# P times v of a pooled attention in eighths of the TensorE array, in float32

## The chip, the cores and the metric

The kernel runs on one core of a Trainium2 chip. The metric is the device time of one execution in microseconds (us); the comparison takes the median of several runs. A core has TensorE (PE; its weight loads are PEld), VectorE (DVE), ScalarE (ACT), GpSimd (POOL) and SyncE (SP), which here issues nearly all transfers. Each engine has its own instruction stream and waits for others by semaphores.

## The reference

Eight batches of attention with eight heads, 576 queries and head dimension 64; keys and values are first averaged over groups of eight positions, so a head has 72 keys. Behind the attention stands a chain of products with weights on all 4608 tokens.

```python
k_p = k.reshape(B, H, 72, 8, 64).mean(axis=3)
v_p = v.reshape(B, H, 72, 8, 64).mean(axis=3)
scores = scale * np.matmul(q, k_p.transpose(0, 1, 3, 2))
attn = softmax(scores)                     # float32
x = np.matmul(attn, v_p)                   # to (4608, 512): heads side by side
out = ((x @ w1) * (x @ w2)) @ w3 @ w_out   # w*: float64
```

## The kernel before

**The weights.** `w3 @ w_out` is formed once (`w_mm`, in 16 steps), which takes the first 85 us of the profiled execution. Every product with weights is done in float32r with a high and a low part of each operand: three passes (high x high, high x low, low x high), `PASSES`. `split` makes the parts: ScalarE casts the high part, VectorE (or GpSimd) subtracts.

**The chunks.** The 4608 tokens are done in 12 chunks of 384 (three tiles of 128). A batch has 576 tokens, so of three chunks one lies over two batches (`pieces` gives the parts: one of 384 columns, or two of 192). For chunk `m` the loop over `j` (8 column blocks) runs `a_mm` and `b_mm` (12 matmuls of 384 columns each, into the PSUM banks `a` and `b`), multiplies them (`b_post`), and `out_mm` adds their product with the folded weights into three banks `o0` to `o2` (9 matmuls of 512 columns). These five banks are the pool `pacc`; the other three are the pool `patt`, tag `att`, used by the whole attention.

**The attention of the next chunk** is threaded through the current one. `s_mm`: scores of a token tile, 16 float32 matmuls with 64 rows and 64 columns of weights, 72 columns streamed, into two `att` banks. `soft1`, `soft2`: row minimum, difference, exp, sum, normalise; for the tiles in `SOFT_ACT` ScalarE does exp with the minimum as bias and the sum as accumulator, otherwise VectorE subtracts first. The result `E` has, for a token, 8 heads x 72 keys. A pair of heads has 144 keys, which is over the 128 rows of the array: 128 of them are handled as a block per pair of heads, and the 2 x 8 that remain go into a small tile `R` (`soft3`), which holds their high and low parts twice each. For P transposed, chunks 0 and 1 use TensorE (`pt_mm`, `ptr_mm`, then `pt_post`, `ptr_post`), later ones VectorE transposes of 32 x 32 (`pt_turn`), a transfer that puts the blocks in place (`pt_move`) and a split into high and low (`pt_split`): `PTh` (high) and `PTx` (low parts, and the transposed `R`).

**The values.** `load_v` and `load_vr` load the pooled rows of v, `prep_v` and `prep_vr` add eight rows on GpSimd (`pool_tree`), and `prep_v2`, `prep_vr1`, `prep_vr2` make high and low parts in block-diagonal tiles `vbd` (two heads, 128 x 128) and `VR`.

**The product `av_mm(n, pr)`** takes one `att` bank for a pair of heads and runs four float32r matmuls with 128 rows into it for each piece:

```python
vh, vl = (vbd[b % 2][s][:, pr] for s in range(2))
nc.tensor.matmul(out=o, lhsT=vh, rhs=PTh[n][:, pr, c], start=True, stop=False)
nc.tensor.matmul(out=o, lhsT=vh, rhs=PTx[n][:, cc, pr], start=False, stop=False)
nc.tensor.matmul(out=o, lhsT=vl, rhs=PTh[n][:, pr, c], start=False, stop=False)
nc.tensor.matmul(out=o, lhsT=VR[b % 2][:, pr], rhs=PTx[n][:, cc, NPR + pr // 2], start=False, stop=True)
```

`av_post(n, pr)` splits the bank into the high and low parts of `xT`, the operand of `a_mm` and `b_mm` of the next chunk.

**The order** is written out by hand: `at(kind, k, fn, ...)` puts a call into slot `k`; a slot holds first loads (`L`), then elementwise work (`P`), weight products (`M`) and attention matmuls (`A`). A `j` step takes three slots, a chunk 24, beginning at `M0 + 24 * m`. Each engine runs its part in that order.

Of the kernel before, what the change touches and what calls it, by code (L numbers as in the profile page):

```python
# [19 lines left out]
def kernel(  # L20
# [55 lines left out]
    nc.vector.tensor_reduce(  # L76
        out=msk,
        in_=ident.rearrange("p (a two e) -> p two a e", two=2, e=2),
        axis=AX.XY,
        op=ALU.add,  # L80
    )
    nc.vector.tensor_tensor(out=msk[:, 0:1], in0=msk[:, 0:1], in1=msk[:, 1:2], op=ALU.subtract)
# [321 lines left out]
    def prep_v(b, hf):  # L404
        if hf == 0:
            vm[b] = p1.tile([P, NPR, D], F32, tag="vm", name="vm")
        pool_tree(stage.pop(("v", b, hf)), vm[b][:, 2 * hf:2 * hf + 2])
# [7 lines left out]
    def prep_vr(b):  # L415
        t = stage.pop(("vr", b))
        m = t[:, :, 0]
        pool_tree(t, m)
        stage["vrp", b] = m

    def prep_vr1(b):
        m = stage["vrp", b]
        hi = p1.tile([P, 2, D], F32R, tag="vrh", name="vrh")
# [4 lines left out]
        stage["vrp", b] = f(hi), m  # L428

    def prep_vr2(b):  # L430
        hi, m = stage.pop(("vrp", b))
        for r in range(4):
            rows = slice(32 * r, 32 * r + 32)
            par = r % 2
# [424 lines left out]
```

## Time and profile before

| | |
|---|---|
| median of 3 runs | 766.41 us (765.66 to 767.91) |
| the profiled execution | 766.73 us, its span 764.9 us |
| mean granted TensorE clock | 0.996 of full speed |
| TensorE busy | 745.8 us (98%) |
| VectorE, ScalarE, GpSimd busy | 443.0, 277.7, 193.2 us |

The span is what the profile shows of the execution. Matmuls are pipelined, so they overlap in the records: the time that one takes in a row of them is the distance of their starts, not their duration.

### The profile page before, as it was taken

Reading aid. Unit: us, or ns where it says so; the run is one execution under the profiler, and the core shown is the slowest. Engines: PE = TensorE matmul, PEld = TensorE weight load, DVE = VectorE, ACT = ScalarE, POOL = GpSimd, SP = SyncE. Lnnn points to the kernel's source line nnn. Section 1 sums busy time; section 2 is a strip of 40 time slices with the busy share of each in tenths; the row PEclk is TensorE's granted clock in tenths of the full one; section 3 lists DMA queues with packets and bytes.
Section 4 is the critical chain, followed back from the end, with each engine's and each line's share of the span. In section 5 each row is a group of like instructions: output and inputs, shape, how many; then the busy total and the mean of one; then the engine's idle time right before and its main releaser. Section 6 shows DMA issues by size and latency. Waiting matters only on the chain.

```text
span 764.9 us, 13065 instructions
## 1 busy us (share of the span) xinstructions
PE 745.8 (98%) x4998; PEld 681.5 (89%) x4998; DVE 443.0 (58%) x874; ACT 277.7 (36%) x670; POOL 193.2 (25%) x229
## 2 busy tenths in 40 slices
PE   8898989999999999999999999999999999999998
PEld 7676878999999999999899999999999899899997
DVE  6976877475485483475574573574574663662211
ACT  5567976232233332222233322232332332322211
POOL 1342666005208500006118500016038300000000
PEclk9999999999999999999999999999999999999999
DMA  9999920027144323037046223145154231210101
GB/s 316 334 286 226 316 37 1 1 79 140 45 122 103 93 84 63 7 109 149 27 116 144 66 59 55 42 95 127 44 136 117 74 67 28 63 42 1 42 1 41
DMA packets 123726, 74.52 MB, mean 97 GB/s; under 512 B 75408, under 2 KB 107408, under 8 KB 123664
## 3 DMA queue, kind: packets, MB, share of 16 engines
q1 hardware_dynamic: 123520, 73.56, 37.4%
q8 instruction: 39, 0.64, 0.4%
q14 instruction: 23, 0.19, 0.1%
q10 hardware_dynamic: 144, 0.13, 0.0%
HBM read 52.43 MB, written 9.44 MB: 81 GB/s over the span
## 4 chain that ended last, share of the span: by engine, by line
PE 84%; DVE 6%; DMA 4%; ACT 4%; issue 1%; SPq 1%; POOL 0%; ACTq 0%
PE a L611 25%; PE b L611 25%; PE o L651 25%; PE att L452 3%; DMA raw<-in_moe_w_out_dram 3%; DMA raw<-in_moe_w_dram 2%; PE att L586 1%; PE att L588 1%; ACT E L478 1%; PE att L587 1%; PE att L585 1%; PE o L681 1%; DVE wb L153 1%; ACT hl L157 1%; DVE hl L158 1%
## 5 line engine op out<-in xcount | busy, mean ns | idle before, releaser
L611 PE MATMUL a<-xT,hl 128*128 128x384 f32 x1152 | 220.4, 339 | 0.4 <-POOL hl L158 0.4
L611 PE MATMUL b<-xT,hl 128*128 128x384 f32 x1152 | 217.9, 337 | 1.9 <-DVE a L631 1.9
L611 PEld LDWEIGHTS a<-xT,hl 128*128 128x128 f32 x1152 | 200.2, 188 | 7.4 <-POOL hl L158 0.7
L611 PEld LDWEIGHTS b<-xT,hl 128*128 128x128 f32 x1152 | 202.0, 189 | 2.2 <-DVE a L631 2.2
L651 PE MATMUL o<-Wc,gh 128*128 128x512 f32 (+1 forms) x576 | 178.8, 391 | 0.0
L397 POOL TENSOR_TENSOR st<-st 128x512 f32<-128x512 f32 (+1 forms) x52 | 71.3, 1371 | 267.3 <-DMA st<-in_k_dram 227.6
L631 DVE TENSOR_TENSOR a<-b,a 128x384 f32<-128x384 f32 x96 | 52.8, 550 | 123.8 <-PE b L611 123.7
L651 PEld LDWEIGHTS o<-Wc,gh 128*128 128x128 f32 x576 | 106.5, 189 | 17.2
L651 PE MATMUL o<-Wc,gl 128*128 128x512 f32 (+1 forms) x288 | 113.2, 393 | 0.0
L632 ACT CAST gh<-a 128x384 fp32r<-128x384 f32 x96 | 49.3, 513 | 166.5 <-DVE a L631 166.5
L621 ACT COPY a<-a 128x384 f32<-128x384 f32 x96 | 45.8, 477 | 111.0 <-PE a L611 100.6
L637 DVE TENSOR_TENSOR gl<-a,gh 128x384 fp32r<-128x384 f32 x96 | 60.2, 627 | 12.8 <-ACT gh L632 12.8
L651 PEld LDWEIGHTS o<-Wc,gl 128*128 128x128 f32 x288 | 54.1, 188 | 12.3
L473 ACT ACTIVATE E<-E 128x288 f32<-128x288 f32 x64 | 28.4, 444 | 96.2 <-DVE E L470 96.1
L597 DVE TENSOR_TENSOR xT<-att,xT 128x384 fp32r<-128x384 f32 x48 | 26.6, 557 | 59.6 <-ACT xT L596 59.6
L474 DVE TENSOR_REDUCE sm<-E 128x4 f32<-128x288 f32 x64 | 29.0, 453 | 36.2 <-ACT E L473 36.2
L681 PE MATMUL o<-hl 128*128 128x512 f32 x144 | 40.6, 415 | 3.2 <-DVE hl L187 3.1
L158 DVE TENSOR_TENSOR PTx<-PTx,PTh 128x512 fp32r<-128x512 f32 x30 | 23.5, 783 | 33.1 <-ACT PTh L157 29.7
L398 POOL TENSOR_TENSOR st<-st 128x256 f32<-128x256 f32 (+1 forms) x52 | 41.3, 794 | 4.1
L413 POOL TENSOR_TENSOR vbd<-vm,vbd 64x256 fp32r<-64x256 f32 x16 | 12.4, 773 | 97.9 <-ACT vbd L412 97.4
L468 DVE TENSOR_REDUCE mx<-att 128x4 f32<-128x288 f32 x72 | 31.8, 442 | 8.8 <-PE att L452 8.8
L681 PEld LDWEIGHTS o<-hl 128*128 128x128 f32 x144 | 26.7, 194 | 9.4 <-DVE hl L187 4.1
(99 smaller groups left out, 774.9 us busy)
## 6 DMA issues: line engine op xcount, KB each, us to landing
raw<-in_moe_w_dram SPq DMA_DIRECT2D x32, 512.0 KB
PTx<-T SPq DMA_DIRECT2D x120, 96.0 KB
out_dram<-ob SPq DMA_DIRECT2D x35, 256.0 KB
st<-in_v_dram SPq DMA_DIRECT2D x16, 512.0 KB
st<-in_k_dram SPq DMA_DIRECT2D x28, 288.0 KB
qs<-in_q_dram SPq DMA_DIRECT2D x112, 48.0 KB
raw<-in_moe_w_out_dram SPq DMA_DIRECT2D x8, 512.0 KB
qs<-in_q_dram SPq DMA_DIRECT2D x96, 24.0 KB
```

The costliest lines, as they stand in the source:

```text
L158: eng.tensor_tensor(out=lo, in0=src, in1=f(hi), op=ALU.subtract)
L397: nc.gpsimd.tensor_tensor(out=t[:, :, 0:4], in0=t[:, :, 0:4], in1=t[:, :, 4:8], op=ALU.add)
L398: nc.gpsimd.tensor_tensor(out=t[:, :, 0:2], in0=t[:, :, 0:2], in1=t[:, :, 2:4], op=ALU.add)
L468: nc.vector.tensor_reduce(out=mx[:nt, hs], in_=sv, axis=AX.X, op=ALU.min)
L474: nc.vector.reduce_sum(out=sm[:nt, hs], in_=E[:nt, hs], axis=AX.X)
L611: nc.tensor.matmul(out=o, lhsT=w12[j, w][sw][:, kt * P:(kt + 1) * P], rhs=x[sx][:, kt], start=(i == 0), stop=(i == 3 * NK - 1))
L621: nc.scalar.copy(out=a, in_=gt[m, j][:, :CH])
L631: nc.vector.tensor_tensor(out=g, in0=ps[:, :CH], in1=g, op=ALU.mult)
L632: nc.scalar.copy(out=gh, in_=g)
L637: nc.vector.tensor_tensor(out=gl, in0=g, in1=f(gh), op=ALU.subtract)
L651: nc.tensor.matmul(out=oacc[m][t][x][:, cols], lhsT=(gh, gl)[sg][:, c], rhs=W[j][sw][:, cols], start=(j == 0 and i == 0), stop=(j == NJ - ...
L681: nc.tensor.matmul(out=wacc[h][it], lhsT=w3t[s][sa][:, it * P:(it + 1) * P], rhs=wo[j][sb], start=(j == 0 and i == 0), stop=(j == NJ - 1 a ...
```

## The change

The product runs in float32 on tiles of 32 rows and 64 columns of the array, eight of them. A head's 72 keys are three parts of 24, each in a row group of 32 (the rest of P is zero there, and v's rows beside it are whatever keys lie there). Four heads stand in the four row groups, and the heads 0 to 3 and 4 to 7 in the two column halves; so a chunk's product is 3 parts x 2 halves x 4 row groups = 24 matmuls for each piece. The four row groups go to four PSUM banks: bank `a` of `pacc` and all three of `att`. `av_mm(n)` is one call in one slot, and four `av_post` follow in the next.

P (the padded tile `EB`, two of them, zeroed once) and v (`vm`) stay in float32: `soft3`, `ptr_mm`, `ptr_post`, `pt_split`, `prep_v2`, `prep_vr`, `prep_vr1`, `prep_vr2` and the mask are gone. In chunks 0 and 1 the six transposes of a tile go in one slot, into two `att` banks (four and two), and are copied by ScalarE and VectorE. v is loaded as three parts of a batch, each by four transfers. The order of rows in `xT` is another (heads `4c + g` in column `g`), so w1 and w2 are loaded with rows permuted, each array by two transfers. Tile (0,1) leaves `SOFT_ACT`. `pt_turn` and `pt_move` come one slot earlier.

```diff
+    KS = 3
+    KW = KP // KS
+    KG = KW - 4
+    EW = 2 * P + 4
...
-    SOFT_ACT = [(0, 0), (0, 1), (0, 2), (1, 1)]
+    SOFT_ACT = [(0, 0), (0, 2), (1, 1)]
...
-    vbd = [[cp.tile([P, NPR, P], F32R, name=f"vbd{i}_{s}") for s in range(2)] for i in range(2)]
-    VR = [cp.tile([P, NPR, P], F32R, name=f"VR{i}") for i in range(2)]
-    msk = cp.tile([P, 2], F32, name="msk")
+    vm = [cp.tile([P, KS, 2, D], F32, name=f"vm{i}") for i in range(2)]
+    EB = [cp.tile([P, KS * EW], F32, name=f"EB{i}") for i in range(2)]
...
-        nc.sync.dma_start(
-            out=raw["w12", j, w].rearrange("p (k c) -> p k c", k=NK),
-            in_=(w1r, w2r)[w][:, 2 * j * P:2 * (j + 1) * P].rearrange("(k p) c -> p k c", p=P))
+        cols = (w1r, w2r)[w][:, 2 * j * P:2 * (j + 1) * P].rearrange("(c g d) x -> c d g x", c=2, g=NK)
+        for c in range(2):
+            nc.sync.dma_start(
+                out=raw["w12", j, w][D * c:D * c + D].rearrange("p (g x) -> p g x", g=NK), in_=cols[c])
...
+    def load_v(b, r):
+        t = stage["v", b, r] = st_tile([P, 2, POOL, D])
+        keys = v[b, :, KG * r * POOL:(KG * r + 32) * POOL].rearrange("(c g) (k e) d -> g k c (e d)", g=4, e=POOL)
+        for g in range(4):
+            nc.sync.dma_start(out=t[32 * g:32 * g + 32].rearrange("p c e d -> p c (e d)"), in_=keys[g])
...
-    def prep_v2(b, par):
-        r = slice(64 * par, 64 * par + 64)
-        hi, lo = (vbd[b % 2][s][r, :, D * par:D * par + D] for s in range(2))
-        nc.scalar.copy(out=hi, in_=vm[b][r])
-        nc.gpsimd.tensor_tensor(out=lo, in0=vm[b][r], in1=f(hi), op=ALU.subtract)
...
+    def prep_v(b, r):
+        pool_tree(stage.pop(("v", b, r)), vm[b % 2][:, r])
+    Et, Mt, PT, xT = {}, {}, {}, {}
+    def parts(E):
+        return E.rearrange("p (r x) -> p r x", x=EW)[:, :, :2 * P].rearrange("p r (h k) -> p h r k", k=32)[:, :, :, :KW]
...
+            Et[n, t] = EB[stage.setdefault("tiles", 0) % 2]
...
+                out=E, in0=sv,
+                in1=mx[:, hs].unsqueeze(2).unsqueeze(3).broadcast_to([P, 4, KS, KW]), op=ALU.subtract)
+            nc.scalar.activation(out=E, in_=E, func=AF.Exp, scale=-1.0)
+            nc.vector.tensor_reduce(out=sm[:, hs], in_=E, axis=AX.XY, op=ALU.add)
...
-        for dup in range(2):
-            nc.scalar.copy(out=R[:nt, :, :, :, dup, 0], in_=er)
-        for dup in range(2):
-            nc.vector.tensor_tensor(
-                out=R[:nt, :, :, :, dup, 1], in0=er, in1=f(R[:nt, :, :, :, dup, 0]), op=ALU.subtract)
...
+    def pt_mm(n, t, lo, hi):
         E = Et[n, t]
-        R = Rt[n, t] = p1.tile([P, NPR, 2, KR, 2, 2], F32R, tag="T" if (n, t) == (0, 1) else "R", name="R")
-        er = E[:nt].rearrange("p (a h) (x e) -> p a (h x) e", h=2, e=KR)[:, :, 0:18:17, :]
-        for dup in range(2):
-            nc.scalar.copy(out=R[:nt, :, :, :, dup, 0], in_=er)
-        for dup in range(2):
-            nc.vector.tensor_tensor(
-                out=R[:nt, :, :, :, dup, 1], in0=er, in1=f(R[:nt, :, :, :, dup, 0]), op=ALU.subtract)
-    Tp = {}
-    def pt_mm(n, t):
-        off, nt = t * P, P
-        E = Et[n, t].rearrange("p (a h) k -> p a (h k)", h=2)
         ps = patt.tile([P, 512], F32, tag="att", name="att")
-        pv = ps.rearrange("p (a c) -> p a c", c=P)
-        for pr in range(NPR):
-            nc.tensor.transpose(
-                out=pv[:, pr, :nt], in_=E[:nt, pr, KR:KR + P], identity=ident[:nt, :nt])
-        Tp[n, t] = pv
-    def ptr_mm(n, t):
-        off, nt = t * P, P
-        R = f(Rt[n, t].rearrange("p a h e u s -> p (a h e u s)"))
-        ps = patt.tile([P, 512], F32, tag="att", name="att")
-        rv = ps[:, :2 * P].rearrange("p (a c) -> p a c", c=P)
-        for g in range(2):
-            nc.tensor.transpose(
-                out=rv[:, g, :nt], in_=R[:nt, g * P:(g + 1) * P], identity=ident[:nt, :nt])
-        Tp[n, t, "r"] = rv
-    def pt_tiles(n):
-        PTh[n] = p1.tile([P, NPR, CH], F32R, tag="PTh", name="PTh")
-        PTx[n] = p1.tile([P, CH // 32, NPR + 2, 32], F32R, tag="PTx", name="PTx")
-    def pt_lo(n, c, w):
-        return PTx[n][:, c.start // 32:c.stop // 32, w].rearrange("p c a i -> p a c i")
-    def turn(out, in_):
+        pv = ps[:, :P * (hi - lo)].rearrange("p (u c) -> p u c", c=P)
+        for u in range(lo, hi):
+            nc.tensor.transpose(out=pv[:, u - lo], in_=E[:, P * u:P * u + P], identity=ident)
+        Tp[n, t, lo] = pv
...
+    def pt_post(n, t, lo, hi, copy):
+        copy(out=pt_tile(n, t)[:, :, lo:hi].rearrange("p c u i -> p u c i"),
+             in_=Tp.pop((n, t, lo)).rearrange("p u (c i) -> p u c i", i=32))
+    def pt_turn(n, t):
+        T = Tp[n, t] = p1.tile([P, 4, NU, 32], F32, tag="T", name="T")
         nc.vector.transpose(
-            out=out.rearrange("p g a i -> p a g i"), in_=in_.rearrange("p a (j g) -> p a g j", g=4))
-    def pt_turn(n, t):
-        off, nt = t * P, P
-        if t == 0:
-            pt_tiles(n)
-        E = Et[n, t].rearrange("p (a h) k -> p a (h k)", h=2)
-        T = Tp[n, t] = p1.tile([P, 4, NPR + 2, 32], F32, tag="T", name="T")
-        turn(T[:nt, :, :NPR], E[:nt, :, KR:KR + P])
-        turn(T[:nt, :, NPR:], f(Rt[n, t][:nt].rearrange("p (g a) h e u s -> p g (a h e u s)", g=2)))
+            out=T.rearrange("p g u i -> p u g i"),
+            in_=Et[n, t][:, :NU * P].rearrange("p (u j g) -> p u g j", u=NU, g=4))
...
-    def pt_split(n, t):
-        off, nt = t * P, P
-        c = slice(off, off + nt)
-        hi, lo = PTh[n][:, :, c].rearrange("p a (c i) -> p a c i", i=32), pt_lo(n, c, slice(0, NPR))
-        split(f(lo), hi, lo)
...
+    def av_mm(n):
+        ps = [pacc.tile([P, 512], F32, tag="a", name="a")]
+        ps += [patt.tile([P, 512], F32, tag="att", name="att") for _ in range(3)]
         for (b, s0, cnt, off) in pieces(n):
-            c, cc = slice(off, off + cnt), slice(off // 32, (off + cnt) // 32)
-            vh, vl = (vbd[b % 2][s][:, pr] for s in range(2))
-            o = ps[:, c]
-            nc.tensor.matmul(out=o, lhsT=vh, rhs=PTh[n][:, pr, c], start=True, stop=False)
-            nc.tensor.matmul(out=o, lhsT=vh, rhs=PTx[n][:, cc, pr], start=False, stop=False)
-            nc.tensor.matmul(out=o, lhsT=vl, rhs=PTh[n][:, pr, c], start=False, stop=False)
-            nc.tensor.matmul(out=o, lhsT=VR[b % 2][:, pr], rhs=PTx[n][:, cc, NPR + pr // 2], start=False, stop=True)
-        Tp[n, pr, "x"] = ps
-    def av_post(n, pr):
-        if pr == 0:
+            cc = slice(off // 32, (off + cnt) // 32)
+            for r in range(KS):
+                for c in range(2):
+                    for g in range(4):
+                        rows = slice(32 * g, 32 * g + 32)
+                        nc.tensor.matmul(
+                            out=ps[g][D * c:D * c + D, off:off + cnt], lhsT=vm[b % 2][rows, r, c],
+                            rhs=PT[n][rows, cc, 2 * r + c], start=(r == 0), stop=(r == KS - 1))
+        Tp[n, "x"] = ps
...
-            at("P", k + 3, soft3, n, t)
             if n > 1:
-                at("P", k + 4, pt_turn, n, t)
-                at("L", k + 5, pt_move, n, t)
-                at("P", pt_at[t], pt_split, n, t)
+                at("P", k + 3, pt_turn, n, t)
+                at("L", k + 4, pt_move, n, t)
                 continue
             k = pt_at[t]
-            at("A", k, pt_mm, n, t)
-            at("A", k + 1, ptr_mm, n, t)
-            at("P", k + 1, pt_post, n, t)
-            at("P", k + 2, ptr_post, n, t)
-        for pr in range(NPR):
-            at("A", av_at[pr], av_mm, n, pr)
-            at("P", av_at[pr] + 1, av_post, n, pr)
+            at("A", k, pt_mm, n, t, 0, 4)
+            at("A", k, pt_mm, n, t, 4, 6)
+            at("P", k + 1, pt_post, n, t, 0, 4, nc.scalar.copy)
+            at("P", k + 1.1, pt_post, n, t, 4, 6, nc.vector.tensor_copy)
+        at("A", av_at, av_mm, n)
+        for g in range(4):
+            at("P", av_at + 1, av_post, n, g)
...
+    def plan_v(b, load, prep):
+        for r in range(KS):
+            at("L", load[r], load_v, b, r)
+            at("P", prep[r], prep_v, b, r)
...
-        s0, ds, pt, av = (3, 4, 5.5, 20.5) if n == 1 else (-1, 3, 9, 16)
+        s0, ds, av = (3, 4, 19) if n == 1 else (-1, 3, 16)
         s_at = [k + s0 + ds * t for t in range(NT)]
-        plan_att(n, s_at, 1, [x + pt for x in s_at], [k + av + pr for pr in range(NPR)])
+        plan_att(n, s_at, 1, [x + 5 for x in s_at], k + av)
...
```

## Rows read from the trace of the kernel before

**Rows 1.** The page, part 1: busy us, share, instructions
```profile
PE 745.8 (98%) x4998; PEld 681.5 (89%) x4998; DVE 443.0 (58%) x874; ACT 277.7 (36%) x670; POOL 193.2 (25%) x229
```

**Rows 2.** Busy time by stretch: us, each engine (instructions), clock, DMA, GB/s
```profile
0.00:85.00 85.00, 74.38 (x465) 60.84 (x465) 63.63 (x114) 56.91 (x146) 30.49 (x40) 0.98 1.05 295
85.00:140.00 55.00, 50.21 (x350) 45.25 (x349) 42.14 (x70) 37.80 (x93) 30.50 (x27) 0.97 0.28 71
140.00:765.00 625.00, 621.25 (x4189) 575.40 (x4187) 337.25 (x691) 182.94 (x432) 132.19 (x162) 1.00 0.30 73
```

**Rows 3.** Timeline of TensorE, 77.5 to 85 us: start, length, count [idle before]
```profile
79.30 0.34 PE L585 MATMUL att<-PTh,vbd 128*128 128x384 f32 x1
...
82.15 1.55 PE L681 MATMUL o<-hl 128*128 128x512 f32 x6
84.21 1.01 PE L305 MATMUL att<-ident,qs 128*128 128x128 f32 x6 [0.51 <-DVE xT L597]
```

**Rows 4.** Timeline of TensorE, 140 to 150 us, a chunk over two batches
```profile
142.18 0.25 PE L585 MATMUL att<-PTh,vbd 128*128 128x192 f32 x1
...
143.06 2.27 PE L611 MATMUL b<-xT,hl 128*128 128x384 f32 x12
```

**Rows 5.** Line 452 (scores) alone by stretch: PE, PEld in work (instructions)
```profile
260.90:260.98 0.08, 0.08 (x4) 0.08 (x8) 1.00 0.00 0
260.98:261.02 0.04, 0.04 (x8) 0.04 (x12) 1.00 0.00 0
```

**Rows 6.** Timeline of TensorE, 60.3 to 61.7 us
```profile
60.41 0.34 PE L452 MATMUL att<-kbd,qT 64*64 64x72 f32 x2 [1.75 <-ACT E L478]
61.61 0.29 PE L452 MATMUL att<-kbd,qT 64*64 64x72 f32 x4 [0.87 <-DVE hl L158]
```

**Rows 7.** Timeline of TensorE, in work from 261.19 and from 261.48
```profile
260.99 0.43 PE L452 MATMUL att<-kbd,qT 64*64 64x72 f32 x16
261.30 0.31 PE L452 MATMUL att<-kbd,qT 64*64 64x72 f32 x8
```

**Rows 8.** Timeline of TensorE, 255 to 330 us
```profile
260.55 0.40 PE L651 MATMUL o<-Wc,gl 128*128 128x512 f32 x1
...
263.72 2.24 PE L611 MATMUL b<-xT,hl 128*128 128x384 f32 x12
...
280.03 0.62 PE L651 MATMUL o<-Wc,gh 128*128 128x512 f32 x2
...
281.89 0.40 PE L651 MATMUL o<-Wc,gl 128*128 128x512 f32 x1
...
284.23 2.24 PE L611 MATMUL b<-xT,hl 128*128 128x384 f32 x12
```

**Rows 9.** Groups by line and form: busy us, mean ns | idle before, releaser
```profile
L597 DVE TENSOR_TENSOR xT<-att,xT 128x384 fp32r<-128x384 f32 x48 | 26.6, 557 | 59.6 <-ACT xT L596 59.6
...
L596 ACT CAST xT<-att 128x384 fp32r<-128x384 f32 x48 | 22.7, 477 | 28.6 <-PE att L588 28.6
```

**Rows 10.** Groups by line and form, elementwise work of P
```profile
L158 DVE TENSOR_TENSOR PTx<-PTx,PTh 128x512 fp32r<-128x512 f32 x30 | 23.5, 783 | 33.1 <-ACT PTh L157 29.7 <-DMA qs<-in_q_dram 3.3
...
L499 ACT CAST R<-E 128x64 fp32r<-128x64 f32 x72 | 16.3, 307 | 26.2 <-DVE E L490 26.2
```

**Rows 11.** Timeline of the SP queue, 83 to 92 us
```profile
84.82 5.50 SPq L392 DMA_DIRECT2D st<-in_v_dram  x6
91.19 0.39 SPq L126 DMA_DIRECT2D raw<-in_moe_w_dram  x1
```

**Rows 12.** Timeline of ScalarE, from 117 us
```profile
120.58 0.66 ACT L135 ACTIVATE wb<-raw 128x512 f32<-128x512 f32 x1
```

**Rows 13.** Waits of TensorE, 85 to 140 us: us in total, times, longest
```profile
PE att L522 <- ACT E L478: 2.5, 1, 2.5
PE b L611 <- DVE a L631: 1.9, 1, 1.9
```

More of the change, by code (lines that the diff above doesn't have):

```diff
@@ L70 @@
     kbd = [cp.tile([P, NPR, KP], F32, name=f"kbd{i}") for i in range(2)]
-    vbd = [[cp.tile([P, NPR, P], F32R, name=f"vbd{i}_{s}") for s in range(2)] for i in range(2)]
-    VR = [cp.tile([P, NPR, P], F32R, name=f"VR{i}") for i in range(2)]
-    msk = cp.tile([P, 2], F32, name="msk")
+    vm = [cp.tile([P, KS, 2, D], F32, name=f"vm{i}") for i in range(2)]
+    EB = [cp.tile([P, KS * EW], F32, name=f"EB{i}") for i in range(2)]
     make_identity(nc, ident)
[L76 to L82, printed above, removed]
     for i in range(2):
-        for s in range(2):
-            nc.gpsimd.memset(vbd[i][s].bitcast(F32), 0.0)
-        nc.gpsimd.memset(VR[i].bitcast(F32), 0.0)
+        nc.gpsimd.memset(EB[i], 0.0)
     def f(ap):
@@ L402, in pool_tree @@
         nc.gpsimd.tensor_tensor(out=dst, in0=x, in1=y, op=ALU.add)
[L404 to L407, printed above, removed]
-    def prep_v2(b, par):
-        r = slice(64 * par, 64 * par + 64)
-        hi, lo = (vbd[b % 2][s][r, :, D * par:D * par + D] for s in range(2))
-        nc.scalar.copy(out=hi, in_=vm[b][r])
-        nc.gpsimd.tensor_tensor(out=lo, in0=vm[b][r], in1=f(hi), op=ALU.subtract)
[L415 to L423, printed above, removed]
-        nc.scalar.copy(out=hi, in_=m)
-        nc.scalar.activation(out=f(hi), in_=f(hi), func=AF.Copy, scale=msk[:, 0:1])
-        nc.scalar.activation(out=m, in_=m, func=AF.Copy, scale=msk[:, 1:2])
[L428 to L434, printed above, removed]
-            nc.gpsimd.tensor_tensor(
-                out=VR[b % 2][rows, r // 2::2, D * par:D * par + D], in0=hi[rows], in1=m[rows], op=ALU.add)
-    Et, Mt, PTh, PTx, xT = {}, {}, {}, {}, {}
+    def prep_v(b, r):
[3 more added lines that the diff above has]
+        return E.rearrange("p (r x) -> p r x", x=EW)[:, :, :2 * P].rearrange("p r (h k) -> p h r k", k=32)[:, :, :, :KW]
     Sp = {}
@@ L462, in soft1 @@
         if half == 0:
[L463 removed]
+            Et[n, t] = EB[stage.setdefault("tiles", 0) % 2]
+            stage["tiles"] += 1
             Mt[n, t] = [p2.tile([P, H], F32, tag=tag, name=tag) for tag in ("mx", "sm")]
[L465 removed]
+        mx, sm = Mt[n, t]
         hs = slice(half, H, 2)
[L467 to L468 removed]
+        E = parts(Et[n, t])[:, hs]
+        sv = Sp.pop((n, t, half))[:, :4 * KP].rearrange("p (h k) -> p h k", k=KP)
+        nc.vector.tensor_reduce(out=mx[:, hs], in_=sv, axis=AX.X, op=ALU.min)
+        sv = sv.rearrange("p h (r k) -> p h r k", r=KS)
         if (n, t) not in SOFT_ACT:
             nc.vector.tensor_tensor(
[L471 to L474 removed]
+                out=E, in0=sv,
+                in1=mx[:, hs].unsqueeze(2).unsqueeze(3).broadcast_to([P, 4, KS, KW]), op=ALU.subtract)
+            nc.scalar.activation(out=E, in_=E, func=AF.Exp, scale=-1.0)
+            nc.vector.tensor_reduce(out=sm[:, hs], in_=E, axis=AX.XY, op=ALU.add)
             return
@@ L490, in soft2 @@
+        nc.vector.reciprocal(out=sm, in_=sm)
         nc.vector.tensor_tensor(
[L491 to L494 removed]
+            out=E, in0=E, in1=sm.unsqueeze(2).unsqueeze(3).broadcast_to([P, H, KS, KW]), op=ALU.mult)
+    Tp = {}
+    NU = 2 * KS
+    def pt_mm(n, t, lo, hi):
         E = Et[n, t]
[L496 to L502 removed]
@@ L547, in pt_move @@
+    def pt_turn(n, t):
+        T = Tp[n, t] = p1.tile([P, 4, NU, 32], F32, tag="T", name="T")
+        nc.vector.transpose(
+            out=T.rearrange("p g u i -> p u g i"),
+            in_=Et[n, t][:, :NU * P].rearrange("p (u j g) -> p u g j", u=NU, g=4))
     def pt_move(n, t):
-        off, nt = t * P, P
-        T = Tp.pop((n, t))
-        for c in range(nt // 32):
+        T, out = Tp.pop((n, t)), pt_tile(n, t)
+        for c in range(4):
             nc.sync.dma_start(
-                out=f(PTx[n])[:, off // 32 + c].rearrange("p a i -> p (a i)"),
-                in_=T[32 * c:32 * c + 32].rearrange("j g a i -> j g (a i)"))
```

87 lines of the change are left out of this document (19 added, 68 removed).

## The prediction

> **What bounds the kernel.** I read the page's busy shares first, then the engines by stage. TensorE is busy 98% of the span [rows 1]. By stage [rows 2]: from 140 us to the end it is busy 621 of 625 us at full clock (2.4 GHz), and what is missing lies behind the last matmul; VectorE has 337 and ScalarE 183 of those 625 us. Before 140 us it lacks 10.6 us (start and weight product, transfers at capacity) and 4.8 us (first token chunk). So a change is worth what it does to TensorE's own work after 140 us, in full, unless it makes a new wait; before that, what it does to the waits.
>
> **P times v before.** A chunk within one batch has 16 matmuls of 384 columns. They run from 79.30 to 82.15 us [rows 3]: 2.85 us, 0.178 each. Each fourth chunk lies over two batches and has 32 of 192 columns; eight take 142.18 to 143.06 [rows 4], 0.88 us or 0.110 each, 3.52 in all. Eight chunks of the one kind and four of the other: 36.9 us.
>
> **P times v after: 24 float32 products a chunk on tiles of 32 rows x 64 columns.** No such tile is in the trace. The nearest is the scores' product, float32 on 64 x 64 tiles, four to the array. Three things are read from it.
>
> *How many run at once.* One call has 16 products and 32 recorded matmuls, two for each. Four are under way by 260.98 us, eight just after [rows 5]: they start in groups of four, one on each tile. At 60.41 us the second tile's bank is not free yet: exactly two run, then the engine stops until 61.61, when four start together [rows 6]. So the two halves of a product stand next to each other in the program, and if the tiles are free, other tiles' first halves overtake a second half. All four tiles work at once.
>
> *What a half costs.* Sixteen are running or to come from the round at 260.99 us, seen at 261.19; eight from the one at 261.30 [rows 7]. The first is the second round of eight (four had started before), the latter the seventh: five rounds in 0.31 us, 62 ns each, 150 clocks at 2.4 GHz for 72 columns. I take that as two clocks a column and 6 over. It could be a floor that has nothing to do with columns; that is the lower bound below.
>
> *What it costs to change to tiles and back.* With a scores call between, the last matmul of the output group starts at 260.55 and the b group at 263.72, 3.17 us; without one, 281.89 to 284.23, 2.34 [rows 8]. The call costs 0.83 us, its eight rounds 0.50, so 0.33 is the change of mode.
>
> The new product has three parts, two column halves, four row groups: eight different tiles follow each other in the program, and each tile gets 3 products, 6 halves. If all eight work at once, a chunk takes 6 rounds of (768 + 6) / 2.4 = 0.3225 us, 1.94 us, or, over two batches, 12 of (384 + 6) / 2.4 = 0.1625, 1.95 us. With 0.33 that is 2.27 and 2.28 us. Saved: 2.85 - 2.27 = 0.58 and 3.52 - 2.28 = 1.24.
>
> The value between the bounds: if only four tiles work at once (all that rows show), a chunk takes 4.20 or 4.23 us; if 62 ns is a floor and a half streams as fast as a float32r matmul of the same length [rows 3, 4], it is 6 x 0.178 + 0.33 = 1.40 or 12 x 0.110 + 0.33 = 1.65. I take eight, because the four that run do not disturb each other (62 ns is what one stream of 144 clocks needs alone), and both ways of splitting, rows and columns, are already among them. The Trainium skill (TensorEngine Tiling, Tiling Modes) lists 32 x 64 with eight independent tiles; no run here shows that.
>
> Eleven chunks lie where TensorE is the bound: 7 x 0.58 + 4 x 1.24 = 9.0 us. Chunk 0's 0.58 us I count as nothing: its product is followed by a wait for the split of its result (0.51 us at 84.21) [rows 3], and now all four banks finish together at the end rather than one by one, so the splits start later by about what the product gains.
>
> **One block in place of four.** The product now takes three banks of `att` and bank `a`, between two a-groups. Bank `a` must be empty before it: the copy out of it (ScalarE, `a_post`) runs during the b group (2.24 us) [rows 8]. It must be empty again for the next a-group: one cast and one subtraction, 0.48 + 0.56 us [rows 9], with an output group as cover on TensorE, whose last matmul starts 1.86 us after its first (280.03 to 281.89) [rows 8], so at least 0.8 us to spare. Gone that cover, an extra 0.1 us on the two engines would cost TensorE 0.1 us in each of 11 chunks. The other three splits follow, and the next chunk reads them only two a, b and output groups later. The scores after it use `att` only from slot 23 on. Nothing.
>
> **Elementwise work.** Removed for each of 36 tiles are two casts of 0.31 us and two subtractions (`soft3`), for 30 of them a subtraction of 0.78 us [rows 10] with its cast, and per batch eight small operations on v's high and low parts with their memsets. Two transposes become one of the same total. After 140 us neither engine bounds: nothing. `pt_turn` and `pt_move` come a slot earlier; the loads behind `pt_move` on the SP queue get no later by that.
>
> **Transfers.** v: 12 instead of 8 per batch, w1 and w2: 32 instead of 16, bytes as before. Six small v transfers take 5.50 us on the SP queue, 0.92 each; at that price a batch costs 11 instead of about 8 us, and 16 more weight loads 15 us at most. The last weight load goes out at 91.19 us [rows 11], and the last conversion reads it from 120.58 us [rows 12]: these 29 us hide a delay of all 15. Without them the 15 us would reach TensorE. I take nothing, and keep 2 us as a bound, since earlier loads may lie closer to their use.
>
> **The filling, before 140 us.** TensorE waits for engines that lose work: 2.5 us for ScalarE's exponentials and 1.9 us for VectorE in chunk 0's stretch [rows 13], 1.75 us for the exponentials of tile (0,1) before 60.41 [rows 6]. Tile (0,1) goes over to VectorE, so its banks are free earlier, and `soft3` and the v casts no longer stand between. Against it: the transposes of a tile now ask for two `att` banks at once where the second came a slot later, and there are three. In chunk 0 the scores of tile 2 then wait for the copy out of the first transposes, and in chunk 1 the second part waits for half 0 of tile (1,1), whose exponentials stay on ScalarE. Bounds: all three waits vanish and 0.4 more, -6 us; each is replaced by one 1 to 1.5 us longer, +4. They nearly balance; I take -0.5.
>
> **Sum.** The profiled execution took 766.73 us (span 764.9), 0.3 over the median of 766.41. 766.7 - 9.0 - 0.5 = 757.2; against the median 756.9.
>
> **Rivals.**
> 1. *Row groups get in each other's way* (the other side). Only two row groups and two banks at once are seen in the scores; here there are four of each. If only four tiles work at once: 12 chunks cost 7 x 1.35 + 4 x 0.71 + 1.35 = 13.6 us more, 780 us. It decides from 36.9 / 12 - 0.33 = 2.74 us a chunk, 0.457 us for a round of eight, that is 5.6 tiles at once. For it: no row shows more than four. Against: the four show no trace of sharing. Chance 0.08.
> 2. *Matmuls start strictly in program order.* Then the second half of each product holds up all tiles, a first half overlaps only the second half ahead of it, and 24 products cost 24 x 0.3225 + 0.33 = 8.07 (48 x 0.1625 + 0.33 = 8.13) us: 12 chunks 97 us, 60 more, 827 us. Against: the scores' 16 products would need 1.0 us, and their rounds take 0.50 [rows 5, 7]. Chance 0.02. The Trainium skill (TensorE: Matmul & The Clock Gate, What overlaps and what doesn't) says that matmuls start and end strictly in program order; by that it would be 827 us, and the trace disagrees with 0.50 us for eight rounds.
> 3. *62 ns is a floor.* Saved then 7 x 1.45 + 4 x 1.87 = 17.6 us: 748.6 us. For it: one column count only. Against: it fits two clocks a column. Chance 0.05.
> 4. *The gain is given back to waits.* A late VectorE makes the a-group after the block wait 0.5 us in 11 chunks, 5.5 us, and the filling loses 3 to 4: 766 us. It needs VectorE to be over 0.8 us late behind the b group's multiplication. Chance 0.07.
>
> My forecast has 0.78; its own range, with the bounds of the filling and the transfers, is 752 to 764. The range of 8 in 10 takes in rival 3 and the nearer part of rival 4: 748 to 766. A measurement of this kernel tells some 0.3% (2.3 us) from no change: faster 0.82 (forecast and rival 3, less the forecast's upper edge), same 0.06, slower 0.12 (rivals 1 and 2, the far end of 4).
>
> **What would show it.** Right: a product block of about 2.0 us, with 48 matmuls (96 over two batches) in six rounds of eight, some 0.32 us apart; the next output group 2.3 us after the b group's end; TensorE still without gaps after the first chunk. Rounds of four or pairs: rival 1 or 2. Rounds 0.18 us apart: rival 3. An a-group that waits for the split of `xT`, or longer waits at 58 and 105 us: rival 4. What would make me wrong above all is a round of eight that takes over 0.45 us.

## The result and the profile after

The changed kernel takes 755.11 us (median of 4 runs, 754.53 to 756.08) against 767.1 of before beside it: a ratio of 0.9847 [0.9826, 0.9868]. The profiled execution took 756.08 us, its span is 754.1. Run again on another chip, the same kernel took 757.63 us (6 runs, 756.05 to 759.34), a ratio of 0.9871 [0.985, 0.9892]. The forecast was 756.9.

The page's busy line, and busy time by stretch as in [rows 2] (after "us", each engine's busy time with its instructions; the last three columns are clock, DMA share, GB/s):

```profile
PE 736.9 (98%) x5510; PEld 659.3 (87%) x5510; DVE 398.1 (53%) x744; ACT 231.1 (31%) x508; POOL 158.4 (21%) x177
```

```profile
0.00:85.00 85.00, 76.41 (x501) 61.51 (x502) 61.83 (x109) 50.76 (x117) 24.98 (x30) 0.94 1.02 284
85.00:140.00 55.00, 50.24 (x439) 44.95 (x438) 39.57 (x68) 36.65 (x85) 26.21 (x21) 1.00 0.40 88
140.00:755.00 615.00, 610.28 (x4574) 552.81 (x4573) 296.73 (x569) 143.71 (x308) 107.23 (x126) 1.00 0.29 74
```

TensorE is the bound as before: after 140 us it lacks 4.7 of 615 us, of which 3.84 lie behind the last matmul and 0.9 behind the end of the span, and there no wait of TensorE shows in either profile, so the 45, 47 and 35 us that VectorE, ScalarE and GpSimd lose over the whole can count only before. After 140 us the gain has to be shorter work of TensorE. Its timeline around a product block, with one bank's matmuls of each round and the next output group:

```profile
181.39 2.24 PE L518 MATMUL b<-xT,hl 128*128 128x384 f32 x12
183.56 0.53 PE L493 MATMUL a<-PT,vm 32*64 32x384 f32 x1
183.57 0.55 PE L493 MATMUL att<-PT,vm 32*64 32x384 f32 x3
183.59 0.53 PE L493 MATMUL a<-PT,vm 32*64 32x384 f32 x1
183.60 0.55 PE L493 MATMUL att<-PT,vm 32*64 32x384 f32 x3
183.94 0.48 PE L493 MATMUL a<-PT,vm 32*64 32x384 f32 x1
...
184.26 0.48 PE L493 MATMUL a<-PT,vm 32*64 32x384 f32 x1
...
185.23 0.48 PE L493 MATMUL a<-PT,vm 32*64 32x384 f32 x1
...
185.68 0.73 PE L558 MATMUL o<-Wc,gh 128*128 128x512 f32 x2
...
187.88 0.86 PE L518 MATMUL a<-xT,hl 128*128 128x384 f32 x4
```

Eight halves start within 0.05 us, one on each tile. The second round follows after 0.37 us, the others 0.32 apart (183.94 to 185.23 are four steps, 0.3225 each). The output group starts 2.12 us after the block's first half.

Where the 10.8 us between the two profiled executions went, from the start of each chunk's first a-group:

| stretch | before, us | after, us | difference |
|---|---|---|---|
| weights, to chunk 0's a-group | 84.98 | 84.11 | -0.87 |
| chunk 0 (with the product of chunk 1) | 64.91 | 62.03 | -2.88 |
| a chunk with a one-batch product | 55.87 | 55.35 | -0.52 |
| a chunk with a two-batch product | 56.33 | 55.08 | -1.25 |
| chunks 1 to 10 together | 558.9 | 551.6 | -7.2 |
| chunk 11 | 52.5 | 52.5 | 0 |
| behind the last matmul | 3.69 | 3.84 | +0.15 |

The weight stage and chunk 0 differ from one execution of a kernel to the next, in part because TensorE's clock falls to the lower level (granted 0.5, 1.2 GHz) in some of their stretches and not in others; the chunks behind them repeat to 0.15 us. One such stretch is in the table: in the profile of before the clock is low for 3.6 us of chunk 0, from 109.8 us on, and in that of the changed kernel it is not; experiment 3, whose waits in front of that place are the changed kernel's, has it again (110 to 120 us; before, changed kernel, experiment 3; the clock is the third number from the end):

```profile
110.00:120.00 10.00, 9.88 (x75) 9.10 (x76) 6.54 (x16) 8.15 (x24) 4.94 (x5) 0.84 0.00 1
110.00:120.00 10.00, 10.00 (x86) 9.21 (x85) 6.67 (x13) 7.92 (x22) 6.36 (x7) 1.00 0.01 2
110.00:120.00 10.00, 10.00 (x74) 9.25 (x74) 6.61 (x12) 7.41 (x21) 5.48 (x7) 0.83 0.01 2
```

### The profile page after: what moved, and what is told of

Its sections match the earlier page's. It is cut to its first block, busy times and chain, and to the rows that moved or that the text cites. A ratio compares the mean times of both kernels' runs of the same rounds, so it can differ in the third digit from the quotient of the medians.

```text
span 754.1 us, 13765 instructions
## 1 busy us (share of the span) xinstructions
PE 736.9 (98%) x5510; PEld 659.3 (87%) x5510; DVE 398.1 (53%) x744; ACT 231.1 (31%) x508; POOL 158.4 (21%) x177
## 4 chain that ended last, share of the span: by engine, by line
PE 92%; DVE 3%; ACT 2%; DMA 1%; SPq 1%; issue 0%; POOL 0%; POOLq 0%; DVEq 0%
PE a L518 27%; PE o L558 26%; PE b L518 26%; PE o L588 4%; PE att L407 3%; PE a L493 3%; SPq L273 1%; DMA qs<-in_q_dram 1%; PE att L207 1%; PE att L213 1%; DMA raw<-in_moe_w_dram 1%; PE a L588 1%; PE att L493 1%; PE att L457 0%; PE b L588 0%
## 5 line engine op out<-in xcount | busy, mean ns | idle before, releaser
L380 POOL TENSOR_TENSOR st<-st 128x512 f32<-128x512 f32 (+1 forms) x52 | 69.7, 1340 | 383.7 <-DMA st<-in_k_dram 260.5
L431 ACT ACTIVATE EB<-EB 128x288 f32<-128x288 f32 x66 | 29.3, 444 | 110.7 <-DVE EB L428 110.7
L432 DVE TENSOR_REDUCE sm<-EB 128x4 f32<-128x288 f32 x66 | 29.9, 453 | 33.7 <-ACT EB L431 33.7
L472 DVE STREAM_TRANSPOSE T<-EB 128x768 f32<-128x768 f32 x30 | 46.6, 1554 | 0.0
L588 PE MATMUL o<-hl 128*128 128x512 f32 x144 | 43.2, 438 | 2.6 <-DVE hl L184 2.6
L407 PEld LDWEIGHTS att<-kbd,qT 64*64 64x64 f32 x1152 | 21.1, 132 | 14.1 <-issue 11.8
L428 DVE TENSOR_TENSOR EB<-att,mx 128x288 f32<-128x288 f32 x66 | 30.2, 458 | 2.3
```

Source lines behind the costliest of these rows:

```text
L380: nc.gpsimd.tensor_tensor(out=t[:, :, 0:4], in0=t[:, :, 0:4], in1=t[:, :, 4:8], op=ALU.add)
L407: nc.tensor.matmul(out=ps[par][x:x + 64, KP * pr:KP * (pr + 1)], lhsT=qT[n][r, pr, t * P + x:t * P + x + 64], rhs=kbd[b % 2][r, pr], start ...
L472: nc.vector.transpose(out=T.rearrange("p g u i -> p u g i"), in_=Et[n, t][:, :NU * P].rearrange("p (u j g) -> p u g j", u=NU, g=4))
L588: nc.tensor.matmul(out=wacc[h][it], lhsT=w3t[s][sa][:, it * P:(it + 1) * P], rhs=wo[j][sb], start=(j == 0 and i == 0), stop=(j == NJ - 1 a ...
```

## The experiments

All edits are to the changed kernel. Times are medians; ratios are to the kernel of before.

**1. The rounds twice.** Each part is multiplied twice. The second pass starts the sum anew, so the output is the same.

```diff
-            for r in range(KS):
+            for r in (0, 1, 2, 0, 1, 2):
```

> Theory (the product itself sets the time, eight tiles at once): a second pass adds 6 rounds of 0.3225 us (12 of 0.1625) and no change of mode, 1.94 us in each of 12 chunks, 23.2 us: 755.1 + 23.2 = 778.3 us. If the product were hidden, or the gain came from the elementwise work alone: 755 to 758. If the change of mode were the larger part of a block (and the rounds less than measured): clearly under 770.

Measured: 779.81 us, 1.0168 [1.0149, 1.0187]. A chunk with a one-batch product takes 57.29 us instead of 55.35: 1.94 for six more rounds, 0.323 a round. The whole is 24.7 us longer than the changed kernel, where the theory had 23.2. The rounds cost what they show. The saving of 0.52 puts the block of the changed kernel at 2.85 - 0.52 = 2.33 us, so what is left for the change to tiles and back is 2.33 - 1.94 = 0.39.

**2. Tile by tile.** The same 24 products, a tile's three parts one behind the other.

```diff
-            for r in range(KS):
-                for c in range(2):
-                    for g in range(4):
+            for c in range(2):
+                for g in range(4):
+                    for r in range(KS):
```

> Same 48 halves, but the six of a tile follow each other in the program. Theory A (a tile keeps a long queue, so other tiles overtake freely): no change, 755 us. Theory B (a tile can keep one half waiting beside the running one, and a third holds up the stream): tiles start 4 rounds apart, 7 x 4 + 6 = 34 rounds in place of 6, 9.0 us more in a chunk, 108 in all: 863 us. Theory C (strict program order, the rule of the Trainium skill, TensorE: Matmul & The Clock Gate, What overlaps and what doesn't): 48 halves less 7 overlaps, 41 rounds, 11.3 us more in a chunk: 890 us.

Measured: 814.31 us, 1.0609 [1.0582, 1.0636], none of the three. The timeline of a block, whole up to 195 us:

```profile
193.51 1.18 PE L493 MATMUL a<-PT,vm 32*64 32x384 f32 x3
194.22 0.53 PE L493 MATMUL att<-PT,vm 32*64 32x384 f32 x1
194.53 0.48 PE L493 MATMUL a<-PT,vm 32*64 32x384 f32 x1
194.59 0.48 PE L493 MATMUL att<-PT,vm 32*64 32x384 f32 x1
194.86 0.48 PE L493 MATMUL a<-PT,vm 32*64 32x384 f32 x1
194.91 0.54 PE L493 MATMUL att<-PT,vm 32*64 32x384 f32 x2
...
200.50 0.73 PE L558 MATMUL o<-Wc,gh 128*128 128x512 f32 x2
```

The block takes 6.99 us instead of 2.12. The first line holds the first tile's halves (bank `a`), 0.37 and 0.32 us apart, the third at 194.21; the second tile's first half starts at 194.22, right behind it, and the third tile's (the second of the x2 line at 194.91) right behind the second's third. A tile has six halves: when the third starts, three wait. So a tile holds three waiting halves besides the one that runs, and a fourth stops the program for all. (Halves come in pairs, so these runs do not tell this from one whole product waiting behind the one at work.) A tile then starts two rounds behind the one before it: 7 x 2 + 6 = 20 rounds, 6.45 us. The first half takes 0.37 us in place of 0.32 on each of the eight tiles, which adds 0.45 in all, and 0.1 lies before the output group: 6.99. Here whole products change order too: the second tile's first product starts at 194.22, the first tile's third one, which stands ahead of it in the program, only at 194.86.

**3. Column half by column half.**

```diff
-            for r in range(KS):
-                for c in range(2):
+            for c in range(2):
+                for r in range(KS):
                     for g in range(4):
```

> All three parts of the first column half, then those of the second: four tiles follow each other in the program. Theory A (long queues): 755 us. Theory B (one half waiting at a tile): the second column half begins 4 rounds late, 10 rounds in place of 6, 1.29 us more in a chunk, 15.5 in all: 770.6 us. Only four tiles at once from start to end: 12 rounds, 1.94 us more, 778 us.

Measured: 765.3 us, 0.9968 [0.995, 0.9986]. The timeline, bank `a` alone:

```profile
186.09 0.53 PE L493 MATMUL a<-PT,vm 32*64 32x384 f32 x1
...
186.47 0.48 PE L493 MATMUL a<-PT,vm 32*64 32x384 f32 x1
...
186.79 0.48 PE L493 MATMUL a<-PT,vm 32*64 32x384 f32 x1
...
186.81 0.53 PE L493 MATMUL a<-PT,vm 32*64 32x384 f32 x1
...
188.91 0.50 PE L558 MATMUL o<-Wc,gh 128*128 128x512 f32 x1
```

The second column half starts (186.81) when the first starts its third round (186.79), again with three waiting, and the block takes 2.82 us: two rounds, 0.70, more. The rule read from experiment 2 gives 6 + 2 = 8 rounds, as seen; my expectation had one waiting half in place of three. By its median this order gives back most of the change's gain, 10.2 us; the twelve blocks are some 8 of them, and chunk 0's stretch at the lower clock is not the order's.

**4. The elementwise work of P put back.** Two casts and two subtractions of 64 columns for each tile, and for the later chunks a cast and a subtraction of 512, on scratch tiles. The small operations on v's parts, and the splits behind the transposes of chunks 0 and 1, are not put back.

```diff
             at("P", k + 2, soft2, n, t)
+            at("P", k + 3, dummy3, n, t)
+            if n > 1:
+                at("P", s_at[t] + 9, dummy_split, n, t)
```

> The elementwise work that was removed from P is put back on ScalarE and VectorE as work that nobody reads (two casts and two subtractions of 64 columns for each tile, a cast and a subtraction of 512 columns for each tile from chunk 2 on), at the places it had. Theory (the steady chunks gain by TensorE's product alone, only the filling by elementwise work): steady chunks keep their 55.1 and 55.35 us, the filling loses 0 to 2 us: 755 to 757 us. Rival (the gain is the elementwise work): most of the 12 us go back, 763 to 767 us.

Measured: 760.42 us, 0.9922 [0.9902, 0.9942], between the two. Where it goes decides: a steady chunk takes 55.42 us (+0.07), chunks 1 to 10 together 1.2 us more, 0.66 of them in chunk 2, where TensorE waits once, 0.4 us, for VectorE; chunk 0 takes 64.75 (+2.72). TensorE's waits for the transposes of this kernel, then of the changed one (us in total, times, longest):

```profile
PE att L457 <- ACT EB L436: 4.5, 1, 4.5
PE att L457 <- DVE EB L428: 3.1, 2, 2.8
```

```profile
PE att L457 <- ACT EB L436: 3.1, 1, 3.1
PE att L457 <- DVE EB L428: 1.4, 1, 1.4
```

So the elementwise work was nearly free after 140 us. Before that, only the first of the two differences is its own. The wait for ScalarE is 3.1 us in the changed kernel's two profiles and in experiments 2, 3, 5 and 6 (1.8 in experiment 1), and 4.5 here alone. The wait for VectorE is 3.0 to 3.7 us in experiments 2, 3 and 11 as well, where nothing was put back (experiment 11 shows what stands behind it). And 1.6 of chunk 0's 2.72 us go with a stretch at the lower clock (0.53 granted from 110.4 to 114.0 us), which experiments 3 and 5 have too. In chunk 0 the elementwise work is therefore worth 1.1 to 1.4 us; that its removal is the gain of the filling is not shown.

**5. Without the output group behind the product.** The product a slot later, directly ahead of the next a-group.

```diff
-        s0, ds, av = (3, 4, 19) if n == 1 else (-1, 3, 16)
+        s0, ds, av = (3, 4, 20) if n == 1 else (-1, 3, 17)
```

> The product one slot later, behind the output group that stood after it, so that the next a-group follows the product directly and needs bank a at once. Theory (the output group covers the split of bank a): each of 11 chunks waits for a cast (0.48 us), a subtraction (0.55) and the hand-overs, 1.2 to 1.4 us, 13 to 15 us in all: 768 to 770 us. If the split were no bound: 755. If VectorE ran late behind the b group's multiplication as rival 4 has it: well over 770.

Measured: 771.57 us, 1.0051 [1.0024, 1.0077], 1.6 us over the upper edge; chunk 0 has a stretch at the lower clock beside its wait (0.53 granted from 110.8 to 114.4 us). The wait is the one that was named (us in total, times, longest):

```profile
PE a L518 <- DVE xT L504: 13.0, 11, 1.2
```

The output group hides 1.2 us in each of 11 chunks, and since it lasts 2.2 (185.68 to 187.88), it has 1.0 to spare. That is the price of the shared bank `a` where nothing stands behind the product.

**6. Tile (0,1) back on ScalarE.**

```diff
-    SOFT_ACT = [(0, 0), (0, 2), (1, 1)]
+    SOFT_ACT = [(0, 0), (0, 1), (0, 2), (1, 1)]
```

> Tile (0,1) goes back to ScalarE's exponentials (SOFT_ACT as before). Theory (its banks then come free later, and TensorE waits for the transposes of tile (0,0) and the scores of tile (0,2)): the start of the first chunk moves from 84.1 by +0.5 to +1.5 us, 755.5 to 756.6 us. Rival (that stretch is held by transfers anyway): no change, 755 us.

Measured: 754.07 us (752.28 to 756.53), 0.9841 [0.9814, 0.9868]. By the times nothing. In the profile the weight stage ends at 80.47 instead of 84.11 us, the other way than the theory had it, while chunk 0 took 1.6 us more, with a stretch at the lower clock (106.8 to 110.2 us). Runs 10 to 12 take this up.

**7. The second pair of transposes a slot later.** In chunk 0 the pair then reads its tile of P after the tile after next has begun to write over it, so a part of P there is another's.

```diff
-            at("A", k, pt_mm, n, t, 4, 6)
+            at("A", k + 1, pt_mm, n, t, 4, 6)
```

(and its copy at `k + 2`.)

> The second two of a tile's six transposes in chunks 0 and 1 go one slot later, as in the kernel before. Theory (two banks asked for at once cost the wait of 3.1 us at 106 us and of 1.4 us at 59 us): an a group of 2.1 us moves into the first wait, chunk 0 gets 1 to 2 us shorter, 753 to 754.5 us. Rival (the exponentials of tile (1,1) end just as late, and another wait follows): no change.

Measured: 755.21 us, 0.9847 [0.9826, 0.9868]. The wait at 109 us is gone, and chunk 0 takes 62.51 us, no less than the 62.03 of the changed kernel. Two new waits of 0.9 us, for VectorE's product `a` and its subtraction (L428), take 1.8 of the 3.1 us back, and TensorE's clock is granted at 0.50 from 91.6 to 95.0 us, where it is 1.00 in the changed kernel: by half speed some 1.7 us (an estimate). So the edit saves some 1.3 us of waits, and the lower clock hides them.

**8. Tile (1,1) to VectorE.**

```diff
-    SOFT_ACT = [(0, 0), (0, 2), (1, 1)]
+    SOFT_ACT = [(0, 0), (0, 2)]
```

> Tile (1,1) leaves ScalarE's exponentials too: VectorE subtracts from its banks. Theory (the bank comes free some 0.7 us sooner, VectorE has 1.8 us more to do in a stretch in which it is busy 8 tenths): chunk 0 between 0.7 us shorter and 0.5 longer, 754.4 to 755.6 us.

Measured: 757.55 us, 0.9871 [0.9849, 0.9893], where I had expected a little under 755.1; it lies within what the changed kernel showed on two chips, so it is no gain, and by the times a loss is not shown. In the profile chunk 0 takes 63.04 us, 1.0 more, at full clock in both. Over the whole run the transposes now wait 5.9 us in four places for VectorE's subtraction, where they had waited 3.1 for ScalarE and 1.4 for VectorE. ScalarE was not the slower engine for this tile.

**9 and 10. All transposes of chunk 0's stretch a slot later, without and with (0,1) on ScalarE.**

```diff
-        plan_att(n, s_at, 1, [x + 5 for x in s_at], k + av)
+        plan_att(n, s_at, 1, [x + (6 if n == 1 else 5) for x in s_at], k + av)
```

> All transposes of chunk 0's stretch come one slot later, so that an a group of 2.1 us stands in front of the pair that waited 3.11 us (at 109.23 us) for the copy of half 0 of tile (1,1) by ScalarE. Theory (that wait is a plain order of slots, and the work put in front of it is free): the wait falls to about 1 us, chunk 0 from 62.0 to 60-61 us, 753 to 754 us in all. Rival (the chain of the other engines paces this stretch, as the run with only the second part later suggested, where the wait went and the time did not): the idle time turns up at other places, chunk 0 stays at 62 to 62.7 us, 755 us in all. A third way: the product of chunk 1 at slot 19 now waits for the last tile's copies, and chunk 0 grows by up to 1 us.

> The same, with tile (0,1) back in SOFT_ACT. By the run with (0,1) alone, that choice is worth nothing measurable, so the same as the run before within 1 us: 753 to 754 us if its theory holds, 755 if not.

Measured: 755.25 us (753.12 to 755.85), 0.9832 [0.9809, 0.9856], and 752.68 (751.61 to 754.51), 0.9805 [0.978, 0.9831]. The timeline of the changed kernel, then of run 9, at the wait:

```profile
105.53 0.60 PE L457 MATMUL att<-ident,EB 128*128 128x128 f32 x4
109.23 0.44 PE L457 MATMUL att<-ident,EB 128*128 128x128 f32 x2 [3.11 <-ACT EB L436]
```

```profile
103.61 2.25 PE L518 MATMUL a<-xT,hl 128*128 128x384 f32 x12
105.70 0.60 PE L457 MATMUL att<-ident,EB 128*128 128x128 f32 x4
107.33 0.44 PE L457 MATMUL att<-ident,EB 128*128 128x128 f32 x2 [1.03 <-ACT EB L436]
```

An a-group fills 2.1 of the 3.1 us, and one new wait of 0.9 takes part of it back (for VectorE's product, as in run 7): chunk 0 takes 61.14 and 61.13 us instead of 62.03. Chunk 0 is close to the theory's 60 to 61 us, while run 9's time is the rival's; run 10 is 2.6 us below it, where I had expected no difference, with ranges that overlap.

**11 and 12. The changed kernel and run 10's, once more, side by side on one chip.**

> The changed kernel as it is, on the same chip as the next one. 755 us (754 to 756.5). Where the profiled execution shows a wait of over 2 us for the first transposes of tile (0,0) and the scores behind them (58 to 63 us), TensorE's clock should be granted at 0.5 right behind it.

> Transposes a slot later in chunk 0's stretch and tile (0,1) back in SOFT_ACT, again. Theory (both together are worth something: the wait at 109 us covered, and no stretch at half clock behind 63 us): 752 to 754 us, 1.5 to 3 us below the run beside it. Rival (the earlier 752.68 was the luck of one chip): within 1 us of it.

Measured: 757.63 us (756.05 to 759.34) and 752.41 (751.13 to 754.0). The changed kernel lies above the 754 to 756.5 us that I had expected of it, so the difference is larger than the 1.5 to 3 us expected. The ranges are 2 us apart: the two edits together are worth 5 us on this chip. TensorE's timeline of the changed kernel here, then of the other:

```profile
58.39 0.63 PE L457 MATMUL att<-ident,EB 128*128 128x128 f32 x4 [0.78 <-DVE EB L428]
61.90 0.51 PE L457 MATMUL att<-ident,EB 128*128 128x128 f32 x2 [2.88 <-DVE EB L428]
63.49 1.55 PE L407 MATMUL att<-kbd,qT 64*64 64x72 f32 x32 [1.07 <-DVE hl L155]
64.96 2.93 PE L588 MATMUL o<-hl 128*128 128x512 f32 x6
```

```profile
57.27 0.66 PE L457 MATMUL att<-ident,EB 128*128 128x128 f32 x4 [0.33 <-ACT EB L436]
58.48 0.44 PE L457 MATMUL att<-ident,EB 128*128 128x128 f32 x2 [0.55 <-ACT EB L436]
59.68 1.04 PE L407 MATMUL att<-kbd,qT 64*64 64x72 f32 x32 [0.76 <-DVE hl L155]
60.65 1.65 PE L588 MATMUL o<-hl 128*128 128x512 f32 x6
```

The stretch from 63 to 68 us, in the changed kernel and in the other:

```profile
63.00:68.00 5.00, 4.51 (x40) 3.65 (x41) 3.47 (x9) 3.08 (x18) 0.00 (x0) 0.50 1.04 221
63.00:68.00 5.00, 5.00 (x27) 3.98 (x26) 2.62 (x6) 4.73 (x17) 0.00 (x0) 1.00 0.97 212
```

With (0,1) on VectorE the transposes and the scores behind them wait 0.78 + 2.88 + 1.07 us, and the six matmuls after that take 2.93 us, almost twice the 1.65 of the other kernel: the granted clock from 63 to 68 us is 0.50. With (0,1) on ScalarE the waits are 0.33 + 0.55 + 0.76 and the clock stays at 1.00. A wait of that length is not always followed by a lower clock: in run 7 TensorE waits 1.46 + 1.28 us at the same place, and the clock from 63 to 68 us is 1.00; the wait of 3.1 us in chunk 0 is followed by a stretch at the lower clock in experiments 2, 3, 5 and 6 and not in the two profiles of the changed kernel. What decides is open. VectorE's timeline in run 11 shows why the subtraction is late; it stands behind an integer operation of the weights:

```profile
59.13 1.77 DVE L150 SCALAR_TENSOR_TENSOR Wc<-Wc 128x512 int32<-128x512 int32 x1
60.82 0.45 DVE L425 TENSOR_REDUCE mx<-att 128x4 f32<-128x288 f32 x1
61.30 0.46 DVE L428 TENSOR_TENSOR EB<-att,mx 128x288 f32<-128x288 f32 x1
```

In the first profile the same L150 took 0.72 us. GpSimd's sum of a k block makes the difference; here it is in run 11, then with L150 in the first profile:

```profile
59.09 1.26 POOL L380 TENSOR_TENSOR st<-st 72x512 f32<-72x512 f32 x1 [2.39 <-DMA st<-in_k_dram]
```

```profile
57.67 1.29 POOL L380 TENSOR_TENSOR st<-st 72x512 f32<-72x512 f32 x1 [2.61 <-DMA st<-in_k_dram]
58.79 0.72 DVE L150 SCALAR_TENSOR_TENSOR Wc<-Wc 128x512 int32<-128x512 int32 x1
```

In both, L150 ends 0.55 us after GpSimd's instruction; in run 11 that instruction has just begun, in the first profile it is almost over. The profiles of all fourteen kernels hold 560 instructions of this operation and shape. The 380 that begin with no GpSimd instruction under way take 0.67 to 0.70 us. Of the 180 that begin during one, 130 take longer, up to 1.82 us, and each of these ends 0.55 us after GpSimd's instruction: VectorE waits for it. (In most of the other 50 it is GpSimd's instruction that takes longer.) Where this L150 took 1.1 to 1.8 us (experiments 2, 3, 4 and 11), the transposes waited 3.0 to 3.7 us for VectorE's subtraction; where it took 0.7 to 0.95 (the first profile, experiments 1, 5, 8 and 9), 1.4 to 2.0.

Chunk 0's a-group started at 80.47, 80.66 and 80.28 us in the three profiled executions with (0,1) on ScalarE, and at 82.17 to 86.24 in the seven others with the product as in the change (runs 4, 5, 7, 8, 9, 11 and the first one).

## Why the prediction was right

**The price of the product.** Right, in mechanism and size. Six rounds of eight 0.3225 us apart, as worked out from two clocks a column and 6 over; 0.39 instead of 0.33 for the change of mode. Saved are 0.52 and 1.25 us a chunk against 0.58 and 1.24; in all 7.2 us in chunks 1 to 10 and 1.2 for the product of chunk 1, 8.5 where the sum had 9.0. The product of chunk 0, which I had counted as nothing, saves 0.84 us more: from its first matmul to chunk 0's a-group it is 5.67 us before (79.30 to 84.97) and 4.83 after (79.28 to 84.11). I had expected the splits behind it to come later; the wait for them (0.51 us [rows 3]) is gone. Rival 1 (row groups in each other's way) and rival 3 (62 ns as a floor) are refuted by the rounds of the changed kernel, and experiment 1 shows that the rounds cost what they show. Rival 2, strict program order, is refuted by eight halves that start within 0.05 us, the first halves of eight products, seven of which overtake second halves. The Trainium skill (TensorE: Matmul & The Clock Gate, What overlaps and what doesn't) has that order; the runs show another, in experiment 2 for whole products too (194.22 before 194.86 us), with a limit: three waiting halves per tile. I did not know the limit, and the sum came out, in this by luck, because the change's order of loops stays inside it. Experiment 3, another order of the same loops, costs 0.70 us a chunk.

**One block in place of four.** Right: no a-group waits for a split after chunk 0. I had counted on at least 0.8 us to spare; by experiment 5 it is 1.0. The first half of rival 4 is thereby refuted for this order; one slot later the wait is there, 1.2 us in each of 11 chunks.

**Elementwise work, transfers.** Right after 140 us, nearly: putting the work back adds 0.07 us to a steady chunk, 1.2 to chunks 1 to 10 together. The 12 v transfers of batch 1 took 3.37 + 2.20 + 2.22 us on the SP queue, 0.65 each, where I had 11 in all at 0.92 each, and no wait for a weight load shows in chunk 0.

**The filling.** This is the term that was mis-sized, and that its net came near is partly luck. I took -0.5 us; the first profile shows -0.87 - (2.88 - 1.25) = -2.5, the second (86.24 and 62.04 us) -0.4, within the bounds of -6 and +4. (The lower bound was added up wrongly: 2.5 + 1.9 + 1.75 and 0.4 more are 6.55.) Of the 2.5 us, 0.84 are chunk 0's product, as said above. The other 1.6, in chunk 0, go with the clock and not with waits: the waits of TensorE there add up to 4.7 us before and 4.8 after, and the changed kernel's chunk 0 takes 62.0 us in the two profiles without the stretch at the lower clock and 63.6 to 63.7 in experiments 3, 5 and 6, which have it (less what the edits of 3 and 5 cost); before, which has it too, 64.91 less the product's 1.25 is 63.7.

That the waits of chunk 0 balance is what I had said, but not as I had said it. VectorE's 1.9 us are gone. The one that I named, in which the second part waits for half 0 of tile (1,1) on ScalarE, is 3.11 us, where 2.5 had stood [rows 13]; this is the longer wait that I had put down as a sign of rival 4. And a wait that I did not have came in: 1.28 us at 90.06, for ScalarE's copy out of bank `a` (`a_post`).

In the weight stage I had one sign wrong. "Tile (0,1) goes over to VectorE, so its banks are free earlier" is the step that failed: VectorE is the later engine there, the waits at 57 to 64 us are 1.41 + 1.17 in the first profile and 0.78 + 2.88 + 1.07 in the second, where 1.75 + 0.87 had stood [rows 6]. With the tile back on ScalarE chunk 0's a-group starts at 80.3 to 80.7 us, 1.5 to 6 us earlier than in the seven profiles with it on VectorE, some of which is clock. Taken back, together with the transposes a slot later, it gives the best kernel of this study, 752.4 to 752.7 us. What the removed elementwise work is worth in the weight stage no run isolates.

## What to carry to other kernels

Price small tiles by rounds: as many tiles as are free start at once, a float32 product is two halves of two clocks a column each. Write the loops so that successive matmuls go to different tiles, with at most three halves waiting on any one (one whole product behind the one at work); a loop over the parts innermost cost three times the block. Where one engine is to relieve another in a filling stage, look at what already stands in its queue there, and at what GpSimd does beside it. A wait of TensorE can cost more than its length where the clock falls behind it; read the clock of the stretch before putting a difference between two profiles down to waits.

## What the hardware showed that I had not expected

- A tile of 32 x 64 takes three float32 halves in waiting besides the one that runs; the next one stops the program for all tiles (experiments 2 and 3, to 0.01 us in both), counted in halves or, as well, in whole products.
- The first half on each tile of a block takes 0.37 us instead of 0.32, also in experiments 1 to 3.
- The rounds do not slow each other at all: eight at once on the whole array step by 0.3225 us, and a tile that works alone at the start of experiment 2 steps by 0.32 (193.89 to 194.21 us).
- One VectorE instruction on 128 x 512 integers took 0.72 us in one execution and 1.77 in another: if it begins during a GpSimd instruction, it can be held until 0.55 us after that one's end. The wait behind it was followed by 5 us at half the clock, and the two executions of one kernel differ by 2.1 us at the end of the weight stage; these are part of it.
